# Set differences in two wide pieces, and another order at the ends of the first halves, in a retention and MLP kernel

## The chip, the cores and the metric

One core of a Trainium2 chip runs the whole kernel. The metric is the device time of one execution in microseconds; "before" has the median of three runs. In the profile, PE is TensorE (PEld its weight loads), DVE is VectorE, ACT is ScalarE, POOL is GpSimd, SP is SyncE, whose queue starts the DMAs.

## The reference

```python
# attention with a decaying state, B=2, H=8, S=768, D=64
for t in range(S):
    state = gamma * state + k[t] v[t]^T          # per batch and head
    y[t] = q[t] state / sqrt(D)
x = y as (1536, 512)
h = x @ moe_w_in;  x = silu(h) @ moe_w_out       # 512 -> 2048 -> 512
h = x @ moe2_w_in; out = max(0.01 h, h) @ moe2_w_out
```

Inputs are float32 values; the weights reach the chip as 64-bit words and are decoded there.

## The kernel before, in words

The 1536 tokens are taken in 12 chunks of 128, the two batches by turns. In the attention a chunk j has scores on TensorE (L244), a mask product on VectorE (`masked`, L251), then values, state part and state update on TensorE (`values`, from L254), and on VectorE the state row (L294). `masked(j + 1)` stands ahead of `store_x(j)` and `state(j)` on VectorE. Three chunks make a set of N = 384 tokens, so there are four sets; sets 0 and 1 belong to p = 0, sets 2 and 3 to p = 1. A set's output is needed by the first layer as high and low halves (`halves`: ScalarE copies to fp32r, VectorE subtracts, L178 and L179), because each matrix product is three products of halves: high x high, high x low, low x high.

Each layer has a first half (512 to 2048) in Q = 8 steps, and a second half (2048 to 512) in 3 x 8 steps of 24 matmuls (L453). A step of the first half multiplies 2 x 2 blocks of weights by 2 x 2 blocks of values with seven products instead of eight (`product`, numbers 1 to 7, each 12 matmuls of 384 columns for both p, L376). It takes sums of weight blocks, formed on GpSimd (`sums`, four 128x256 operations, L175), and differences of values between the even and the odd set of a pair p. Of these, L318 and L319 form two on VectorE as soon as a chunk of the odd set is there, and `rest_t` two more on GpSimd over the whole set (L324, L325, 768 columns). `split_t` makes halves of them: 1536 columns on ScalarE and VectorE. Step 0 of a layer (`begin`, L627) does plain blocks instead, 4 blocks x 2 pairs of 12 matmuls (L648), while the differences are still being made; then `n.go(1)` is the first product of step 1. In `rest` (L659) the products of a step stand in a given sequence; `copy` (ScalarE, L405) and `add` (VectorE, L409) collect them, `act` (L418, L420) applies the activation, `keep` (L425) writes the step's output to DRAM scratch, from which `fetch_g` (L441) brings it back for the second half, into `sf` and three tiles `ct`. `split_g` makes its halves.

Weights take five operations before use: `words` (ScalarE, L131 and L133), `clamp` (VectorE, L137 and the mask L141), `sign` (L148), `low` (L155), and the halves. `split_a` and `split_s` are the halves of plain blocks and of sums. Lists of tasks (`up_tasks`, L563; `behind`, L530) say which of these go ahead of which product.

The order is that of the code: engines and the SP queue take their instructions strictly in line, and each instruction waits on semaphores for what it needs. PSUM has four pairs of banks; a pair is a place of one product or of two outputs. The chunk loop ends at L559, the layers' loop follows at L683, and `finish_x` (L458) makes the values of layer 1 from the outputs of layer 0, through `put_first` and `put_second`.

## Time and profile before

| | |
|---|---|
| median of 3 runs | 579.21 us (578.32 to 582.25) |
| profiled execution | 580.35 us, its span 578.6 us |
| mean granted TensorE clock | 0.987 |
| PE busy | 555.2 us, 96% of the span |
| DVE busy | 342.6 us, 59% |
| ACT busy | 282.7 us, 49% |
| POOL busy | 104.4 us, 18% |
| HBM | 80.82 MB read, 37.75 MB written |

The profile is one execution. A busy share is the time an engine spent in its instructions; the chain that ended last is the work followed back from the last instruction through what released each step: 83% of it is TensorE, 6% VectorE, 5% DMA. A row of the timeline gives a start from the span's beginning, a duration, engine, line, operation with output and inputs, their shapes, and how many instructions it joins; in brackets stands how long the engine was idle before, and what released it. Rows of busy time by line and form give the count, the busy time and the mean of one.

### The profile page before, as it was taken

The page shows a single profiled execution, that of the slowest core. Times are in us where ns is not written, and L with a number is a line of the kernel's source. Part 1 is how long each engine was busy: PE and PEld are TensorE (multiplying, and loading weights), DVE is VectorE, ACT ScalarE, POOL GpSimd, SP SyncE. Part 2 cuts the span into 40 slices and gives each one's busy share as a digit, 9 for nine tenths or more (in the row PEclk, how much of TensorE's full clock was granted, in tenths as well). Part 3 has the DMA queues.
Part 4 walks back from the last instruction along what each step waited for, and adds up shares of the span by engine and source line. Part 5 has one row for each costly group of instructions (what it writes and reads, how often), then busy time and mean ns, then how long its engine had stood idle before and what let it go on. Part 6 is the DMA issues. An engine that isn't in the chain of part 4 may idle for free.

```text
span 578.6 us, 7971 instructions
## 1 busy us (share of the span) xinstructions
PE 555.2 (96%) x3246; PEld 498.1 (86%) x3246; DVE 342.6 (59%) x354; ACT 282.7 (49%) x330; POOL 104.4 (18%) x94
## 2 busy tenths in 40 slices
PE   8887979999998999999999899999999999999997
PEld 6776979999997888888888799999998888888885
DVE  4888866888865486676673756666655562212300
ACT  2223566777766565634622565566665453213201
POOL 2675433333300000000200532222200000000000
PEclk9988979999999999999999999999999999999999
DMA  8973216687876957878582075777627782532401
GB/s 323 392 269 116 73 36 219 228 290 283 289 257 237 374 188 215 292 228 311 189 260 105 0 261 175 249 258 252 223 110 290 283 293 94 167 109 84 137 0 73
DMA packets 35129, 119.09 MB, mean 206 GB/s; under 512 B 3218, under 2 KB 3346, under 8 KB 33044
## 3 DMA queue, kind: packets, MB, share of 16 engines
q1 hardware_dynamic: 34800, 118.24, 58.8%
q8 instruction: 25, 0.41, 0.3%
q10 hardware_dynamic: 292, 0.34, 0.2%
q14 instruction: 12, 0.10, 0.1%
HBM read 80.82 MB, written 37.75 MB: 205 GB/s over the span
## 4 chain that ended last, share of the span: by engine, by line
PE 83%; DVE 6%; DMA 5%; ACT 3%; POOL 1%; issue 1%; SPq 0%; DVEq 0%; ACTq 0%
PE p L453 44%; PE p L376 33%; DMA sf<-g 3%; DMA att_a<-att_dram 3%; PE p L648 2%; DVE w L179 2%; POOL sf L175 1%; PE p L273 1%; PE p L264 1%; ACT w L178 1%; PE p L244 1%; DVE c L251 1%; DVE r L155 1%; DVE big L318 1%; DVE big L319 1%
## 5 line engine op out<-in xcount | busy, mean ns | idle before, releaser
L376 PE MATMUL p<-tt,w 128*128 128x384 f32 x672 | 126.3, 340 | 3.7 <-ACT c L405 3.7
L376 PEld LDWEIGHTS p<-tt,w 128*128 128x128 f32 x672 | 119.4, 190 | 5.3 <-ACT c L405 5.2
L179 DVE TENSOR_TENSOR w<-c,w 128x1024 fp32r<-128x1024 f32 x46 | 56.2, 1224 | 90.2 <-ACT w L178 90.1
L453 PE MATMUL p<-w,wt 128*128 128x512 f32 x432 | 98.4, 389 | 0.0
L453 PE MATMUL p<-wt,w 128*128 128x512 f32 x432 | 98.4, 389 | 0.0
L453 PEld LDWEIGHTS p<-wt,w 128*128 128x128 f32 x432 | 81.1, 188 | 16.8
L453 PEld LDWEIGHTS p<-w,wt 128*128 128x128 f32 x432 | 81.1, 188 | 16.8
L178 ACT ACTIVATE w<-c 128x1024 fp32r<-128x1024 f32 x46 | 48.4, 1061 | 60.0 <-DMA c<-g 34.4
L453 PE MATMUL p<-w,w 128*128 128x512 f32 x288 | 67.3, 391 | 1.8 <-DVE w L179 1.0
L376 PE MATMUL p<-xa,w 128*128 128x384 f32 x336 | 64.3, 341 | 2.1 <-ACT big L418 2.1
L453 PEld LDWEIGHTS p<-w,w 128*128 128x128 f32 x288 | 53.8, 188 | 14.3 <-DVE w L179 2.2
L376 PEld LDWEIGHTS p<-xa,w 128*128 128x128 f32 x336 | 59.8, 190 | 2.5 <-ACT big L418 2.5
L409 DVE TENSOR_TENSOR big<-p,c 128x768 f32<-128x768 f32 x42 | 40.1, 954 | 32.3 <-PE p L376 19.8
L405 ACT ACTIVATE c<-p 128x768 f32<-128x768 f32 x42 | 34.1, 812 | 48.7 <-PE p L376 48.6
L175 POOL TENSOR_TENSOR sf<-r 128x256 f32<-128x256 f32 x28 | 33.9, 1232 | 115.6 <-DVE r L155 61.1
L133 ACT ACTIVATE u<-ws 128x1024 int32<-128x1024 uint32 x32 | 36.4, 1137 | 22.5 <-DVE r L155 22.5
L155 DVE CUSTOM_DVE_ANT_0 r<-r,u 128x2048 uint16<-128x2048 uint16 x32 | 41.2, 1289 | 0.9 <-ACT u L133 0.5
L131 ACT ACTIVATE r<-ws 128x1024 f32<-128x1024 f32 x32 | 36.6, 1143 | 9.7 <-DMA scr<-r 5.5
L179 DVE TENSOR_TENSOR w<-sf,w 128x1024 fp32r<-128x1024 f32 (+1 forms) x18 | 21.7, 1205 | 32.8 <-ACT w L178 32.8
L148 DVE SCALAR_TENSOR_TENSOR r<-ws,r 128x1024 int32<-128x1024 int32 x32 | 39.6, 1236 | 0.7
L324 POOL TENSOR_TENSOR big<-big 128x768 f32<-128x768 f32 x4 | 7.3, 1832 | 169.1 <-DVE big L319 169.1
L179 DVE TENSOR_TENSOR w<-r,w 128x768 fp32r<-128x768 f32 (+1 forms) x20 | 23.5, 1175 | 14.5 <-ACT w L178 14.5
(86 smaller groups left out, 566.0 us busy)
## 6 DMA issues: line engine op xcount, KB each, us to landing
ws<-w_dram SPq DMA_DIRECT2D x64, 512.0 KB, 5.7
g<-big SPq DMA_DIRECT2D x16, 1536.0 KB, 5.8
c<-g SPq DMA_DIRECT2D x46, 512.0 KB, 6.8
att_a<-att_dram SPq DMA_DIRECT2D x18, 512.0 KB, 6.4
scr<-r SPq DMA_DIRECT2D x18, 512.0 KB, 6.4
r<-scr SPq DMA_DIRECT2D x18, 512.0 KB, 7.4
att_b<-att_dram SPq DMA_DIRECT2D x6, 512.0 KB, 8.3
out_dram<-big SPq DMA_DIRECT2D x11, 256.0 KB, 2.1
```

Of the source, the lines that this page charges most:

```text
L131: nc.scalar.activation(out=r.bitcast(F32), in_=t[:, :, :, 1].bitcast(F32), func=AF.Abs)
L133: nc.scalar.activation(out=u, in_=t[:, :, :, 0].bitcast(U32), func=AF.Copy, scale=2.0 ** -29)
L148: nc.vector.scalar_tensor_tensor(out=r, in0=t[:, :, :, 1], scalar=-0x40000000, in1=r, op0=ALU.bitwise_and, op1=ALU.bitwise_or)
L155: nc.vector.tensor_tensor(out=r, in0=r, in1=u, op=ALU.add)
L175: nc.gpsimd.tensor_tensor(out=o, in0=a, in1=b, op=op)
L178: nc.scalar.activation(out=h, in_=s, func=AF.Copy)
L179: nc.vector.tensor_tensor(out=l, in0=s, in1=h.bitcast(F32), op=ALU.subtract)
L376: nc.tensor.matmul(out=o, lhsT=a[:, ta, k * 128:k * 128 + 128], rhs=rhs(p, tb, k), start=(begin and m == 0), stop=(end and m == 5), skip_g ...
L405: nc.scalar.activation(out=ct[n][:, c, 0:N], in_=self.X[:, c, 0:N], func=AF.Copy)
L409: nc.vector.tensor_tensor(out=self.block(f, half, lanes), in0=t[:, c, 0:N], in1=ct[n][:, c, 0:N], op=ALU.add)
L453: nc.tensor.matmul(out=y, lhsT=l, rhs=r, start=(i == 0 and f == 0 and n == 0), stop=(i == Q - 1 and f == 1 and n == 2),)
L648: nc.tensor.matmul(out=places[m][:, p, 0:N], lhsT=a[:, ta, r, k * 128:k * 128 + 128], rhs=x, start=(n_ == 0), stop=(n_ == 11), skip_group_ ...
```

## The change: what it does

1. The differences L318 and L319 are no longer formed chunk by chunk from PSUM. For the odd sets ScalarE copies the chunk's whole output to `tm` after the halves (chunk 5 on; up to chunk 4 VectorE writes the product with the gate straight into the target), and `first_t` then takes both differences over 768 columns with operands in SBUF: for p = 0 on GpSimd at chunk 10, for p = 1 on VectorE at the first block of layer 0. `rest_t(0)` moves to chunk 11, `rest_t(1)` behind the sums of the first block of layer 0. In even sets from chunk 5 on the copy comes after the halves instead of ahead of them. `finish_x` does all halves and then all copies of one output half after the other, and the differences at the end.
2. In `begin` the second pair's blocks stand in another sequence, and the first product of the next step with its copy goes ahead of the last block. The tasks of layer 0's first step are in another order.
3. In the last step of a first half the sequence is 6, 2, 7, 5, 4, 3, and the first fetches and halves of the second half stand earlier.

```diff
--- before.py
+++ after.py
@@ -301,23 +301,19 @@
         return t
 
 
-    def put_first(s, a, b, ys):
+    def put(s, a, b, k):
         p = s // 2
-        f = xf[p][:, :, :, a:b]
-        h, l = (xa[p][:, n].rearrange("p (a k) n -> p a k n", a=2)[:, :, :, a:b] for n in range(2))
-        for i, y in enumerate(ys):
-            halves(h[:, i], l[:, i], y)
-        for i, y in enumerate(ys):
-            nc.scalar.activation(out=f[:, i], in_=y, func=AF.Copy)
-
-    def put_second(s, a, b, ys):
-        p = s // 2
-        f, t = xf[p][:, :, :, a:b], tm[p][:, :, :, a:b]
-        h, l = (xb[p][:, n, :, a:b] for n in range(2))
-        halves(*(t[:, :, a:b] for t in b12[p]), ys[0])
-        nc.vector.tensor_tensor(out=t[:, 0], in0=ys[0], in1=f[:, 0], op=ALU.subtract)
-        nc.vector.tensor_tensor(out=t[:, 1], in0=ys[1], in1=t[:, 0], op=ALU.subtract)
-        halves(h, l, ys[1])
+        if s % 2 == 0:
+            h, l = (xa[p][:, n, 2 * k:2 * k + 2, a:b] for n in range(2))
+            return h, l, xf[p][:, k, :, a:b]
+        h, l = ((b12[p], [xb[p][:, n] for n in range(2)])[k][n][:, :, a:b] for n in range(2))
+        return h, l, tm[p][:, k, :, a:b]
+
+
+    def first_t(p, e):
+        f, t = xf[p], tm[p]
+        e.tensor_tensor(out=t[:, 0], in0=t[:, 0], in1=f[:, 0], op=ALU.subtract)
+        e.tensor_tensor(out=t[:, 1], in0=t[:, 1], in1=t[:, 0], op=ALU.subtract)
 
     def rest_t(p):
         f, t = xf[p], tm[p]
@@ -333,24 +329,18 @@
         a, b = c * C, c * C + C
         y = yu[j][0]
         g4 = lambda t: t.rearrange("p (a k i) -> p a k i", a=2, k=2)
-        kept = False
+        y = g4(y)
+        f = (tm if s % 2 else xf)[s // 2][:, :, :, a:b]
         if j < LATE:
-            kept = s % 2 == 0
-            n = j % 2
-            yg = xf[s // 2][:, :, :, a:b] if kept else sf[:, 2 * n:2 * n + 2].rearrange(
-                "p a (k i) -> p a k i", k=2)
-            nc.vector.tensor_tensor(out=yg, in0=g4(y), in1=g4(G), op=ALU.mult)
-            y = yg
+            nc.vector.tensor_tensor(out=f, in0=y, in1=g4(G), op=ALU.mult)
+            y = f
+        if s % 2 == 0:
+            halves(*(xa[s // 2][:, n].rearrange("p (a k) n -> p a k n", a=2)[:, :, :, a:b] for n in range(2)), y)
         else:
-            y = g4(y)
-        if s % 2 == 0:
-            f = xf[s // 2][:, :, :, a:b]
-            h, l = (xa[s // 2][:, n].rearrange("p (a k) n -> p a k n", a=2)[:, :, :, a:b] for n in range(2))
-            if not kept:
-                nc.scalar.activation(out=f, in_=y, func=AF.Copy)
-            halves(h, l, y)
-        else:
-            put_second(s, a, b, [y[:, 0], y[:, 1]])
+            for k in range(2):
+                halves(*put(s, a, b, k)[0:2], y[:, k])
+        if j >= LATE:
+            nc.scalar.activation(out=f, in_=y, func=AF.Copy)
 
 
     TERMS = ((0, 0), (0, 1), (1, 0))
@@ -456,13 +446,18 @@
             )
 
     def finish_x(s, ya, yb):
-        at = s * T
-        while at < s * T + T:
-            e = min(s * T + T, (at // N + 1) * N)
-            n, a = at // N, at % N
-            c = slice(at - s * T, e - s * T)
-            (put_first if n % 2 == 0 else put_second)(n, a, a + e - at, [ya[:, :, c], yb[:, :, c]])
-            at = e
+        for k, y in ((1, yb), (0, ya)):
+            todo = []
+            at = s * T
+            while at < s * T + T:
+                e = min(s * T + T, (at // N + 1) * N)
+                n, a = at // N, at % N
+                todo.append((y[:, :, at - s * T:e - s * T], *put(n, a, a + e - at, k)))
+                at = e
+            for i, h, l, _ in todo:
+                halves(h, l, i)
+            for i, _, _, f in todo:
+                nc.scalar.activation(out=f, in_=i, func=AF.Copy)
 
     def finish_out(s, m, y):
         j = s * (T // C) + m
@@ -531,7 +526,7 @@
             2: lambda: load_next(), 5: lambda: load_next(),
             4: lambda: words(wa), 6: lambda: clamp(wa), 7: lambda: signed(wa),
             8: lambda: low(wa), 9: lambda: split_a(wa),
-            10: lambda: (rest_t(0), words(wb)), 11: lambda: (rest_t(1), clamp(wb), signed(wb)),
+            10: lambda: (first_t(0, nc.gpsimd), words(wb)), 11: lambda: (rest_t(0), clamp(wb), signed(wb)),
         }
         places = [place(p) for p in range(2)]
         for j in range(NJ):
@@ -566,13 +561,13 @@
             if layer == 0 and k < 2:
                 wd = first_w[3]
                 if k == 0:
-                    at(0, lambda: split_t(0, 0), lambda: low(wb))
-                    at(1, lambda: sums(wb), lambda: split_t(1, 0))
-                    at(2, lambda: split_a(wb))
-                    at(3, lambda: split_t(0, 1), lambda: words(wc))
-                    at(4, lambda: split_s(wb))
-                    at(5, lambda: split_t(1, 1))
-                    at(6, lambda: clamp(wc), lambda: signed(wc))
+                    at(0, lambda: low(wb), lambda: first_t(1, nc.vector), lambda: sums(wb))
+                    at(0, lambda: split_t(0, 0), lambda: rest_t(1))
+                    at(1, lambda: split_a(wb), lambda: split_t(1, 0))
+                    at(3, lambda: split_s(wb), lambda: words(wc))
+                    at(4, lambda: split_t(0, 1))
+                    at(5, lambda: split_t(1, 1), lambda: clamp(wc))
+                    at(6, lambda: signed(wc))
                     at(7, lambda: low(wc), lambda: sums(wc))
                 else:
                     at(0, lambda: split_a(wc))
@@ -605,7 +600,7 @@
             w = second_w[1][k]
             n, m = (first_w[Q + k + d] if k + d < Q else None for d in (1, 2))
             if k == 0:
-                at(0, lambda: split_t(1, 0), lambda: fetch_w(n))
+                at(0, lambda: fetch_w(n), lambda: split_t(1, 0))
                 at(2, lambda: split_a(n), lambda: words(w))
                 at(4, lambda: sums(n), lambda: clamp(w))
                 at(5, lambda: signed(w), lambda: fetch_w(m))
@@ -652,25 +647,28 @@
                             n_ += 1
                     if p == 1:
                         s.act(f, half, places[m])
+                    if p == 1 and at == 2:
+                        n.go(1)
+                        n.copy(0)
                 put_back[p]()
-            n.go(1)
-            n.copy(0)
 
         def rest(s, n, before, tasks):
-            seq = (6, 2, 5, 7, 1, 4, 3) if n else (6, 2, 5, 7, 0, 4, 3)
+            seq = (6, 2, 5, 7, 1, 4, 3) if n else (6, 2, 7, 5, 4, 3)
             for m, p in enumerate(seq):
                 if m == 2:
                     if before.i:
                         before.act(0, 1)
+                    if n is None:
+                        fetch_g(s.layer, 0, 1)
                     before.keep()
-                if p == 7:
+                if m == 3:
                     s.act(0, 0)
                 for t in tasks[m]:
                     t()
                 if p == 1:
                     n.go(1)
                     n.copy(0)
-                elif p:
+                else:
                     s.go(p)
                 if p == 6:
                     s.copy(1)
@@ -678,8 +676,9 @@
                     s.add(0, 0, 0, s.Z)
                 elif p == 7:
                     s.copy(2)
+                if m == 3:
                     s.add(1, 1, 2, s.V)
-                elif p == 4:
+                if p == 4:
                     s.act(1, 1)
                     s.act(1, 0, s.X)
                 elif p == 3:
@@ -694,16 +693,16 @@
                 s, n = steps[k], steps[k + 1]
                 if k == 0:
                     begin(s, n, tasks, ((0, 1, 2, 3), (1, 3, 0, 2))[layer],
-                          ((1, 0, 2, 3), (2, 0, 1, 3))[layer], put_back)
+                          ((0, 1, 2, 3), (0, 2, 1, 3))[layer], put_back)
                     s.done()
                     continue
                 if n is None:
                     ahead = second_w[layer][:2]
-                    tasks[2] += [lambda: fetch_g(layer, 0, 0), lambda: fetch_g(layer, 0, 1)]
-                    tasks[3] += [lambda: fetch_w(ahead[0])]
-                    tasks[4] += [lambda: split_g(layer, 0, 0), lambda: fetch_g(layer, 0, 2)]
-                    tasks[5] += [lambda: fetch_w(ahead[1])]
-                    tasks[6] += [lambda: split_g(layer, 0, 1)]
+                    tasks[1] += [lambda: split_g(layer, 0, 0)]
+                    tasks[2] += [lambda: fetch_w(ahead[0])]
+                    tasks[4] += [lambda: fetch_g(layer, 0, 2), lambda: fetch_w(ahead[1]), lambda: split_g(layer, 0, 1)]
+                elif k == Q - 2:
+                    tasks[4] += [lambda: fetch_g(layer, 0, 0)]
                 rest(s, n, steps[k - 1], tasks)
             steps[Q - 1].act(0, 1)
             fetch_g(layer, 0, 3)
@@ -791,6 +790,7 @@
                         put_back[1] = lambda: free.append(last_place)
                     finish_x(s, ya, yb)
                     if s:
+                        first_t(s - 1, (nc.gpsimd, nc.vector)[s - 1])
                         rest_t(s - 1)
                 elif end_:
                     for m in range(4):
```

On VectorE, in chunks 8 and 9 of the attention (p_555, now p_550, is the output of chunk 9, `gst` the state). Before:

```order
L294 TENSOR_TENSOR gst<-gst,p_512 128x256 [waits Pool_49]
L155 ISA r_74<-r_74,u 128x2048 [waits DVE_49]
L251 TENSOR_TENSOR c_70<-p_544,c_69 128x1024 [waits PE_49]
L179 TENSOR_TENSOR w_87<-p_555,w_87 128x2x128 [waits Activation_49]
L318 TENSOR_TENSOR big<-p_555,big 128x2x128
L319 TENSOR_TENSOR big<-p_555,big 128x2x128 [waits DVE_49]
L179 TENSOR_TENSOR xb_67<-p_555,xb_67 128x2x128 [waits Activation_49]
L294 TENSOR_TENSOR gst<-gst,p_555 128x256 [waits Pool_49]
L179 TENSOR_TENSOR w_88<-r_74,w_88 128x1024 [waits Activation_49]
L251 TENSOR_TENSOR c_71<-p_591,c_69 128x1024 [waits PE_49]
```

Now:

```order
L294 TENSOR_TENSOR gst<-gst,p_507 128x256 [waits Activation_49,Pool_49]
L155 ISA r_74<-r_74,u 128x2048 [waits DVE_49]
L251 TENSOR_TENSOR c_70<-p_539,c_69 128x1024 [waits PE_49]
L179 TENSOR_TENSOR w_87<-p_550,w_87 128x2x128 [waits Activation_49]
L179 TENSOR_TENSOR xb_67<-p_550,xb_67 128x2x128 [waits Activation_49]
L294 TENSOR_TENSOR gst<-gst,p_550 128x256 [waits Activation_49,Pool_49]
L179 TENSOR_TENSOR w_88<-r_74,w_88 128x1024 [waits DVE_49,Activation_49]
L251 TENSOR_TENSOR c_71<-p_585,c_69 128x1024 [waits PE_49]
```

The two differences are gone, and the state rows wait for ScalarE as well as for GpSimd; that wait is for the copy of the same output.

On ScalarE, in the start of layer 0 (`w_659` and `w_651` are halves of sums, `tt_658` and `tt_650` those of the second pair's differences, `big<-p` the silus of the blocks). Before:

```order
L178 ACTIVATE w_89<-r_75 128x768 [waits DVE_49]
L178 ACTIVATE tt_85<-big 128x2x768 [waits Pool_49]
L131 ACTIVATE r_76<-ws_72 128x1024 [waits DMAHW7_49,DMAHW6_49]
L133 ACTIVATE u<-ws_72 128x1024 [waits Activation_49]
L178 ACTIVATE w_659<-sf 128x1024 [waits Pool_49]
L418 ACTIVATE big<-p_662 128x2x384 [waits DVE_49,PE_49]
L178 ACTIVATE tt_658<-big 128x2x768
L418 ACTIVATE big<-p_661 128x2x384 [waits PE_49]
L418 ACTIVATE big<-p_663 128x2x384 [waits PE_49]
L418 ACTIVATE big<-p_664 128x2x384 [waits PE_49]
L405 ACTIVATE c_69<-p_794 128x2x384 [waits PE_49]
```

Now:

```order
L178 ACTIVATE w_89<-r_75 128x768 [waits DVE_49]
L178 ACTIVATE tt_650<-big 128x2x768 [waits DMAHW4_49,DMAHW5_49,DMAHW3_49,DMAHW6_49,DMAHW2_49,DMAHW7_49,DVE_49,Activation_49]
L178 ACTIVATE w_651<-sf 128x1024 [waits Pool_49]
L131 ACTIVATE r_76<-ws_72 128x1024 [waits DMAHW7_49,DMAHW6_49]
L133 ACTIVATE u<-ws_72 128x1024
L178 ACTIVATE tt_85<-big 128x2x768
L408 ACTIVATE big<-p_653 128x2x384 [waits DVE_49,PE_49]
L178 ACTIVATE tt_650<-big 128x2x768 [waits Pool_49]
L408 ACTIVATE big<-p_654 128x2x384 [waits PE_49]
L408 ACTIVATE big<-p_655 128x2x384 [waits PE_49]
L395 ACTIVATE c_69<-p_772 128x2x384 [waits PE_49]
L408 ACTIVATE big<-p_656 128x2x384 [waits PE_49]
```

The first silu stood behind the halves of the sums; now the halves of both pairs' differences `tt_85` and `tt_650` stand around it, and the copy of the next product (L395) stands ahead of the last silu.

On GpSimd, the end of the attention and the start of layer 0 (`att_b` is the last chunk's input, `r_75` the first weights). Before:

```order
L222 TENSOR_TENSOR att_b<-att_b,gst 128x512 [waits DMAHW4_49,PE_49]
L324 TENSOR_TENSOR big<-big 128x768 [waits Activation_49]
L325 TENSOR_TENSOR big<-big 128x768
L324 TENSOR_TENSOR big<-big 128x768 [waits DVE_49,Activation_49]
L325 TENSOR_TENSOR big<-big 128x768
L175 TENSOR_TENSOR sf<-r_75 128x256 [waits DVE_49]
L175 TENSOR_TENSOR sf<-r_75 128x256
L175 TENSOR_TENSOR sf<-sf,r_75 128x256 [waits Pool_49]
L175 TENSOR_TENSOR sf<-r_75,sf 128x256 [waits Pool_49]
```

Now:

```order
L222 TENSOR_TENSOR att_b<-att_b,gst 128x512 [waits DMAHW4_49,PE_49]
L315 TENSOR_TENSOR big<-big 128x768 [waits Activation_49]
L316 TENSOR_TENSOR big<-big 128x768 [waits Pool_49]
L320 TENSOR_TENSOR big<-big 128x768 [waits Pool_49]
L321 TENSOR_TENSOR big<-big 128x768
L175 TENSOR_TENSOR sf<-r_75 128x256 [waits DVE_49]
L175 TENSOR_TENSOR sf<-r_75 128x256
L175 TENSOR_TENSOR sf<-sf,r_75 128x256 [waits Pool_49]
L175 TENSOR_TENSOR sf<-r_75,sf 128x256 [waits Pool_49]
L320 TENSOR_TENSOR big<-big 128x768 [waits DVE_49,Activation_49]
L321 TENSOR_TENSOR big<-big 128x768
```

L315 and L316 are the new wide differences, L320 and L321 are `rest_t`: that of the second pair moved from ahead of the four sums to behind them.

## Rows read from the trace of the kernel before

**Rows 1.** The page's line of TensorE's granted clock: 40 slices of 14.5 us, tenths.
```profile
PEclk9988979999999999999999999999999999999999
```

**Rows 2.** TensorE's waits: line waited for, us in total, times, longest us.
```profile
PE p L264 <- DVE c L251: 7.0, 4, 2.8
PE p L376 <- ACT c L405: 3.7, 4, 1.0
...
PE p L648 <- DVE xb L179: 2.7, 1, 2.7
```

**Rows 3.** Windows: bounds, us, busy by engine, granted clock, DMA share, GB/s.
```profile
80.00:84.00 4.00, 3.10 (x10) 2.59 (x10) 3.90 (x5) 2.07 (x3) 0.00 (x0) 0.50 0.01 4
322.00:330.00 8.00, 5.33 (x31) 5.04 (x31) 6.67 (x6) 4.99 (x5) 4.77 (x3) 1.00 0.00 0
```

**Rows 4.** Timeline, one mask operation at two places: start us, us, engine, line, operation.
```profile
63.00 2.22 DVE L141 TENSOR_SCALAR r<-r 128x1024 int32<-128x1024 int32 x1
...
177.92 0.69 DVE L141 TENSOR_SCALAR r<-r 128x1024 int32<-128x1024 int32 x1
```

**Rows 5.** Groups by line and form: count, busy us, mean ns, idle before.
```profile
L318 DVE TENSOR_TENSOR big<-sf,big 128x256 f32<-128x256 f32 x2 | 2.8, 1375 | 0.0
L319 DVE TENSOR_TENSOR big<-sf,big 128x256 f32<-128x256 f32 x2 | 1.6, 786 | 0.1
L318 DVE TENSOR_TENSOR big<-p,big 128x768 f32<-128x768 f32 x1 | 0.9, 948 | 0.0
L324 POOL TENSOR_TENSOR big<-big 128x768 f32<-128x768 f32 x4 | 7.3, 1832 | 169.1 <-DVE big L319 169.1
L178 ACT ACTIVATE tt<-big 128x1536 fp32r<-128x1536 f32 x8 | 11.6, 1478 | 0.0
```

**Rows 6.** Timeline, attention: ScalarE's copy of an output, and the last mask product.
```profile
44.84 0.60 ACT L350 ACTIVATE big<-p 128x512 f32<-128x512 f32 x1 [2.67 <-PE p L281]
...
53.88 1.22 DVE L251 TENSOR_TENSOR c<-p,c 128x1024 f32<-128x1024 f32 x1
```

**Rows 7.** Timeline, start of layer 0, several engines.
```profile
66.40 1.75 DVE L179 TENSOR_TENSOR tt<-big,tt 128x1536 fp32r<-128x1536 f32 x1
68.07 1.22 DVE L155 CUSTOM_DVE_ANT_0 r<-r,u 128x2048 uint16<-128x2048 uint16 x1
...
75.26 0.73 POOL L175 TENSOR_TENSOR sf<-r,sf 128x256 f32<-128x256 f32 x1
...
77.83 3.44 PE L376 MATMUL p<-xa,w 128*128 128x384 f32 x12 [2.14 <-ACT big L418]
...
85.93 2.26 PE L376 MATMUL p<-xa,w 128*128 128x384 f32 x12
```

**Rows 8.** Timeline, ends of the two first halves (layers 0 and 1).
```profile
176.01 1.12 ACT L133 ACTIVATE u<-ws 128x1024 int32<-128x1024 uint32 x1
176.13 4.35 PE L376 MATMUL p<-tt,w 128*128 128x384 f32 x24
...
187.85 8.50 PE L453 MATMUL p<-w,w 128*128 128x512 f32 x36 [0.76 <-DVE w L179]
...
433.54 4.35 PE L376 MATMUL p<-tt,w 128*128 128x384 f32 x24
...
443.78 6.60 PE L453 MATMUL p<-w,w 128*128 128x512 f32 x26 [0.25 <-DVE w L179]
```

**Rows 9.** Timeline, start of layer 1, several engines.
```profile
318.56 0.38 ACT L178 ACTIVATE xa<-p 128x256 fp32r<-128x256 f32 x1 [0.97 <-PE p L453]
...
319.72 0.81 ACT L178 ACTIVATE w<-p 128x768 fp32r<-128x768 f32 x1
...
323.52 1.82 POOL L324 TENSOR_TENSOR big<-big 128x768 f32<-128x768 f32 x1 [42.34 <-DVE big L319]
...
332.61 1.60 POOL L175 TENSOR_TENSOR sf<-r,sf 128x256 f32<-128x256 f32 x1
...
341.15 2.38 PE L376 MATMUL p<-tt,w 128*128 128x384 f32 x12 [0.90 <-ACT c L405]
```

## The prediction, made before the changed kernel ran

> **What bounds the kernel now.** I read the slices first. TensorE is busy in nearly every one, and the line of its granted clock stays at 9 outside three slices [rows 1]: products at full clock fill the program, and time can be won or lost only where TensorE waits or runs at half clock. The waits of TensorE say where that is [rows 2]: on the mask product of VectorE in the attention (7.0 us), on copies by ScalarE in the product steps (3.7 us), and once on a low half of VectorE (2.7 us). The edits touch four such places: the attention with the start of layer 0, the last step of layer 0, the start of layer 1, its last step. The rest of the program moves as a block.
>
> Two facts of the trace set the prices. The first is the clock. In 80 to 84 us it was 0.50, the 1.2 GHz level, after TensorE had stood 2.14 us in front of a product [rows 3, 7]; in 322 to 330 us it was 1.00, the 2.4 GHz level, though 2.67 of the 8 us were idle [rows 3]. So some waits cost a stretch at half clock on top and some don't. The second is that VectorE and GpSimd hold each other up: the same mask of a word tile (L141) took 2.22 us while GpSimd subtracted and 0.69 us with GpSimd idle [rows 4]. A chunk's difference with both inputs in SBUF took 1375 ns as a mean [rows 5]. The Trainium skill has a rule for this ("SBUF — State Buffer", section "Who interferes with whom"): a VectorE instruction with two SBUF inputs and a GpSimd instruction that reads SBUF lock each other out for a whole instruction, and one with a PSUM input is free of that. It speaks against this change, which replaces differences from PSUM by differences of two SBUF operands.
>
> **The sum.** All times are on the profiled execution's scale, 580.35 us, of which 578.6 is the span; the median of the three runs is 1.14 lower.
>
> *Attention.* The two-operand differences of chunks 3 and 4 go: 2 x (1.375 + 0.786) = 4.3 us [rows 5]. They stood ahead of the state row and the next mask product on VectorE. One low half then waits out part of a GpSimd product, so I take -4.1. In return ScalarE copies a whole output from chunk 5 on, 0.60 us each [rows 6], behind its halves, and the state row on VectorE, which before waited for GpSimd alone, now waits for that copy too; behind the state row the next mask product is queued, and for that TensorE waits. In chunk 5 copy and removed differences cancel (-0.2); in 6, 7 and 8 it costs 0.6 each (+1.9); in 9 about half (+0.3). The wide differences on GpSimd at chunk 10 can catch a VectorE instruction for up to one of their 1.83 us [rows 5]: half of that, +0.9. The last mask product, which ended at 55.10 [rows 6], ends at 53.9: -1.2, between -3.7 and -0.4.
>
> *Start of layer 0 up to the low words.* From the last mask product to the end of the low words (69.29) [rows 7] passed 14.2 us. Out of this go four differences, a 1.75 us low half of a set [rows 7], and the hold on the masks of the words (1.53 on L141 by [rows 4], about 1 on the clamp before it, an estimate from the same two rows); two ScalarE copies come in at 0.60. That leaves 9.5 us: -4.7.
>
> *From there to the first product of the next step.* Here the cover is gone. Behind the low words now stand, all with SBUF operands and so one after the other on VectorE and GpSimd: two wide differences (0.95 each, [rows 5]), four sums (0.73, [rows 7]), two low halves of sets (1.75), two remaining differences (1.83, [rows 5]) and two low halves of weights (about 1.2, as the low words): 14.4 us. Each starts some 0.07 before the last ends (66.40 + 1.75 against 68.07), so 13.6. ScalarE takes its orders in line: the silu that frees the first product's PSUM place stands behind the high half of the last difference, so 1.48 [rows 5] and 0.8 for the silu follow (768 columns, as [rows 9]): 15.9. Before it was 77.83 - 69.29 = 8.5: +7.4. Moving the product ahead of the last block does not fill the gap, since the product itself waits for that silu. It starts at 79.3 and not at 77.83.
>
> By the skill's rule that issue order decides who blocks, VectorE would win where it asks first, and the window would be 12.5, the sum 1.1 lower. No row shows an order of that kind beyond strict alternation, so I keep 13.6.
>
> *From that product on.* Before, 8.1 us passed from 77.83 to the third product at 85.93 [rows 7], 3.0 of them by the half clock, for two products of 2.1 and a copy of 0.9. Now three pieces go there (product, block, product), 6.3, and the copy is covered. The clock will fall again, for the wait is about 7 us. The least that a slice at 8 tenths stands for is 1.5 us lost [rows 1]; the most seen here is 3.0. I take 2.5: 8.8, +0.7. Start of layer 0 and attention in all: +2.2, between -2.4 (mask product at its low end, 1.5 lost, issue order) and +3.5.
>
> *Last step of layer 0.* From 176.13 four products should end at 184.5; the run of the second half starts at 187.85 [rows 8], so 3.1 are lost, to a copy between two products and to the halves of the first fetched values. The new order puts another product between copy and overwrite, and fetches a step earlier. New is that product 3 waits for an add on VectorE, behind the low half of the fetched values, the masks and the signs. ScalarE's word pass ends at 177.13 [rows 8] and the half behind it at 178.2; then 1.2, 0.95, 0.69, 0.69, 1.2 and the add's 0.95 on VectorE give 183.9, against 182.4 when TensorE gets there: 1.5 of wait. Net -1.6, between -3.1 and -0.5.
>
> *Last step of layer 1.* Same reading: 433.54 + 8.4 = 441.9, the run starts at 443.78 after one lone product [rows 8], about 1.5 lost. Here the words stand behind the fetched values and the add is early: -1.5, between -1.5 and 0.
>
> *Start of layer 1.* The first difference on GpSimd started at 323.52, since each piece was finished in turn. Now all halves and copies of both outputs come first: per output, ScalarE and VectorE by turns with 0.38, 0.43, 0.81 and 0.96, then copies of 0.39 and 0.81, 3.8 us, twice with handovers 7.9 from 318.56 [rows 9]; the 768-wide half of 0.81 is in the rows, the 256-wide ones are the first row of the group and near it. Then two wide differences on VectorE, 1.9: GpSimd starts at 328.4, 4.9 later. From there 11.1 us of exclusive work as above (two differences 3.7, one low half 1.75, weights 0.95, sums 2.9, masks 1.4, signs 1.2, less overlaps 0.8) end at 339.5; they ended at 334.21 [rows 9]. Then 1.05 + 1.48 + 0.81 + 0.81 on ScalarE: product 6 at 343.7, against 341.15: +2.5. TensorE has the product and the last block to fill with, and still idles about 4.8 us in front of product 6. That lies between 2.67 idle, after which the clock stayed, and 7, so half clock costs 0 to 3.0, and I take 1.6: +4.1.
>
> The sum is +2.2 - 1.6 - 1.5 + 4.1 = +3.2: 583.6 on the profile's scale, **582.4 against the median**, +0.6%. About 1% is what a measurement of this kernel can tell from no change, that is 573.4 to 585.0. All terms low give 574.7, all high 587.7.
>
> **Rivals.**
>
> *The shared work isn't one after the other (faster), 0.20.* If GpSimd's long operations ran beside VectorE's, only their own chain would count: low words at 63.4, then sums 2.9 and differences 3.7, then 1.48 and 0.8: the product starts at 72.2, the clock holds, and the next step's second piece of work, at 85.93 before, is reached at 78.5: -7.4. In layer 1, 328.4 + 3.7 + 2.9 + 4.2 = 339.2: -2.0 and no half clock. With -1.6 and -1.5 that is -12.5: 567.9, 566.7 against the median. For it speaks that a mean in the rows mixes calm and crowded cases; against it speak the two times of L141 [rows 4].
>
> *Both new waits cost a full stretch at half clock (slower), 0.27.* The place is the three pieces behind the 7 us wait in layer 0, and the product behind the 4.8 us wait in layer 1. If all 6.3 us behind the first run at 1.2 GHz, that is 3.8 more than I took, and 3.0 behind the second is 1.4 more: 588.8, 587.6 against the median. For it speaks that 2.14 us of waiting was enough once [rows 3]; against it, that 2.67 was not. It is slower by over 1% from 2.6 us of half clock loss above my 4.1.
>
> *The forecast, 0.53.* Its upper terms alone reach past 585.0 in a tenth of its cases, and its lower ones below 573.4 in fewer.
>
> The range is 570 to 589: it takes in both ends of the forecast and the slower rival and leaves out most of the faster one. Faster by over 1%: 0.20 + 0.03 = 0.23. Slower: 0.27 + 0.06 = 0.33, within 1%: 0.44.
>
> **What the changed profile would show.** The last mask product ends near 53.9. Between the low words and the first silu of layer 0, VectorE and GpSimd alternate without overlap for some 13 us, and TensorE shows one wait of about 7 us in front of the first product (by the line of ACT's silu); if that wait is under 3, the faster rival holds. The clock's fall behind it lasts 3 to 6 us; over 7 is the slower one. In the last step of layer 0 product 3 waits 1.5 for an add. In layer 1 GpSimd's differences start near 328, product 6 near 343.7 less what was won before. I would be wrong altogether if a DMA, which I took as in time everywhere, were the last to come: the fetches moved a step earlier stand on SP's queue ahead of others.

## The result, and the profile after

The change makes the kernel slower: 588.12 us (median of 4, 587.3 to 588.73) against 579.95 for the kernel before beside it, a ratio of 1.0137 with the interval 1.0098 to 1.0176. The profiled execution took 588.43 us, its span 586.6 us, 8.0 more than before. The granted clock is no explanation by itself: 0.985 against 0.987, and the page's line answers to [rows 1].

```profile
PEclk9998979999999999999999999999999999999999
```

TensorE's waits after, as in [rows 2]:

```profile
PE p L264 <- issue: 5.8, 3, 4.4
PE p L366 <- ACT big L408: 4.6, 1, 4.6
PE p L366 <- ACT c L395: 4.0, 2, 3.7
PE p L443 <- DVE w L179: 2.4, 2, 1.6
...
```

A row with `issue` has no releaser in the profile; its longest wait, 4.4 us, ends where the last mask product of the attention does (54.41 and 54.31 us). In its second halves the kernel before had three short waits (L443 is what L453 was), all at the start: 0.70 and 0.76 us in layer 0, 0.25 in layer 1 [rows 8]. Now there is a row of them, and their place is seen when TensorE's runs of layer 0's second half are set side by side. Before (start us, us, what, how many; idle before and its end):

```profile
186.59 0.49 PE L453 MATMUL p<-w,w 128*128 128x512 f32 x1 [0.70 <-ACT w L178]
187.85 10.99 PE L453 MATMUL p<-w,w 128*128 128x512 f32 x47 [0.76 <-DVE w L179]
198.68 32.80 PE L453 MATMUL p<-w,wt 128*128 128x512 f32 x144
...
242.20 32.80 PE L453 MATMUL p<-w,wt 128*128 128x512 f32 x144
...
285.72 32.80 PE L453 MATMUL p<-w,wt 128*128 128x512 f32 x144
```

After:

```profile
188.21 11.04 PE L443 MATMUL p<-w,w 128*128 128x512 f32 x48
199.71 0.81 PE L443 MATMUL p<-w,wt 128*128 128x512 f32 x2 [0.46 <-ACT wt L178]
201.16 16.68 PE L443 MATMUL p<-w,wt 128*128 128x512 f32 x72 [0.64 <-DVE wt L179]
218.30 16.20 PE L443 MATMUL p<-w,wt 128*128 128x512 f32 x70 [0.46 <-DVE wt L179]
234.34 11.04 PE L443 MATMUL p<-w,w 128*128 128x512 f32 x48
246.06 0.50 PE L443 MATMUL p<-w,wt 128*128 128x512 f32 x1 [0.68 <-ACT w L178]
247.31 32.69 PE L443 MATMUL p<-w,wt 128*128 128x512 f32 x143 [0.76 <-DVE w L179]
...
298.53 27.27 PE L443 MATMUL p<-w,wt 128*128 128x512 f32 x119 [1.65 <-DVE w L179]
```

Three unbroken sets of 43.5 us became three broken ones. With the same marks in both traces (start of a named run, after minus before) the 8.0 us fall apart so:

| stretch | shift at its end | its own share |
|---|---|---|
| attention and start of layer 0, to the third product (85.93, now 87.64) | +1.7 | +1.7 |
| layer 0's steps, to the last step (176.13, now 178.44) | +2.3 | +0.6 |
| last step of layer 0, to the second half (187.62 without its lone first matmul, now 188.21) | +0.6 | -1.7 |
| second half of layer 0 (318.36, now 325.63) | +7.3 | +6.7 |
| start of layer 1, to its third product (343.37, now 353.51) | +10.1 | +2.9 |
| steps of layer 1, to the last step (433.54, now 443.85) | +10.3 | +0.2 |
| last step of layer 1 (443.55 without its lone first matmul, now 452.21) | +8.7 | -1.7 |
| to the end | +8.0 | -0.7 |

The largest share lies in a stretch for which the forecast had no term. The first two rows set one execution against one: profiles of runs with the same code up to there reach the second half of layer 0 up to 1.7 us apart (187.36 us in e5, 189.06 in e1), so these two shares are known no better than that.

### The profile page after: what moved, and what is told of

The parts are those of the page before. It is cut to its first block, busy times and chain, and to the rows that moved or that the text cites. A ratio compares the mean times of both kernels' runs of the same rounds, so it can differ in the third digit from the quotient of the medians.

```text
span 586.6 us, 7977 instructions
## 1 busy us (share of the span) xinstructions
PE 557.8 (95%) x3246; PEld 499.8 (85%) x3246; DVE 342.8 (58%) x340; ACT 288.0 (49%) x340; POOL 116.0 (20%) x98
## 4 chain that ended last, share of the span: by engine, by line
PE 59%; DVE 12%; DMA 10%; ACT 8%; issue 6%; POOL 4%; SPq 0%; ACTq 0%; DVEq 0%; POOLq 0%
PE p L366 30%; PE p L443 27%; DMA c<-g 5%; DVE r L155 3%; DMA att_a<-att_dram 2%; ACT w L178 2%; DVE w L179 2%; POOL sf L175 2%; DMA att_b<-att_dram 1%; DMA scr<-r 1%; DVE r L141 1%; DVE r L148 1%; DVE r L137 1%; POOL big L321 1%; DVE xa L179 1%
## 5 line engine op out<-in xcount | busy, mean ns | idle before, releaser
L179 DVE TENSOR_TENSOR w<-c,w 128x1024 fp32r<-128x1024 f32 x46 | 57.6, 1256 | 97.8 <-ACT w L178 97.6
L443 PE MATMUL p<-w,wt 128*128 128x512 f32 x432 | 100.3, 391 | 4.7 <-DVE w L179 2.4
L443 PEld LDWEIGHTS p<-w,wt 128*128 128x128 f32 x432 | 80.6, 188 | 24.2 <-DVE w L179 3.6
L443 PE MATMUL p<-wt,w 128*128 128x512 f32 x432 | 98.4, 389 | 0.0
L443 PEld LDWEIGHTS p<-wt,w 128*128 128x128 f32 x432 | 81.1, 188 | 16.8
L443 PE MATMUL p<-w,w 128*128 128x512 f32 x288 | 66.3, 389 | 0.0
L443 PEld LDWEIGHTS p<-w,w 128*128 128x128 f32 x288 | 54.0, 188 | 11.1
L395 ACT ACTIVATE c<-p 128x768 f32<-128x768 f32 x42 | 34.0, 811 | 44.7 <-PE p L366 44.6
L155 DVE CUSTOM_DVE_ANT_0 r<-r,u 128x2048 uint16<-128x2048 uint16 x32 | 42.8, 1339 | 0.9 <-ACT u L133 0.7
L179 DVE TENSOR_TENSOR w<-sf,w 128x1024 fp32r<-128x1024 f32 x16 | 21.3, 1329 | 33.1 <-ACT w L178 33.1
L179 DVE TENSOR_TENSOR w<-r,w 128x768 fp32r<-128x768 f32 (+1 forms) x20 | 26.2, 1312 | 16.7 <-ACT w L178 16.7
L366 PE MATMUL p<-xb,w 128*128 128x384 f32 x168 | 31.7, 337 | 1.2 <-DVE big L399 1.2
```

The costliest lines, as they stand in the source:

```text
L155: nc.vector.tensor_tensor(out=r, in0=r, in1=u, op=ALU.add)
L179: nc.vector.tensor_tensor(out=l, in0=s, in1=h.bitcast(F32), op=ALU.subtract)
L366: nc.tensor.matmul(out=o, lhsT=a[:, ta, k * 128:k * 128 + 128], rhs=rhs(p, tb, k), start=(begin and m == 0), stop=(end and m == 5), skip_g ...
L395: nc.scalar.activation(out=ct[n][:, c, 0:N], in_=self.X[:, c, 0:N], func=AF.Copy)
L443: nc.tensor.matmul(out=y, lhsT=l, rhs=r, start=(i == 0 and f == 0 and n == 0), stop=(i == Q - 1 and f == 1 and n == 2),)
```

## The experiments

The median of every run with the ratio to the kernel before, which ran beside it:

| run | us | ratio (95%) |
|---|---|---|
| the change | 588.12 | 1.0137 (1.0098 to 1.0176) |
| e1_old_finish | 581.16 | 1.002 (1.0001 to 1.0038) |
| e2_keep_first | 586.52 | 1.0109 (1.0076 to 1.0143) |
| e3_old_last | 588.9 | 1.0151 (1.0111 to 1.0191) |
| e4_split_late | 588.63 | 1.0145 (1.0107 to 1.0182) |
| e5_first_vec | 587.72 | 1.0135 (1.0104 to 1.0166) |
| e6_only_last_kf | 576.68 | 0.9948 (0.9923 to 0.9974) |
| e7_finish_keep | 578.42 | 0.997 (0.9948 to 0.9992) |
| e8_no_first0 | 586.17 | 1.011 (1.0072 to 1.0148) |
| e9_by_piece | 578.2 | 0.9936 (0.9916 to 0.9957) |
| e10_ahead | 576.42 | 0.991 (0.9888 to 0.9933) |
| e11_state_first | 586.79 | 1.0095 (1.0068 to 1.0122) |
| e12_hybrid | 575.1 | 0.9923 (0.99 to 0.9947) |

**e1_old_finish: layer 1's values formed as before.**

```diff
     def finish_x(s, ya, yb):
-        for k, y in ((1, yb), (0, ya)):
...
+            (put_first if n % 2 == 0 else put_second)(n, a, a + e - at, [ya[:, :, c], yb[:, :, c]])
...
-                        first_t(s - 1, (nc.gpsimd, nc.vector)[s - 1])
```

> The change, but with the kernel before's way of forming layer 1's values: each piece with its two differences at once on VectorE from PSUM, no wide differences there. Theory 1: the second half of layer 0 loses 6.7 us at three separate places, 2.4 by a late train of fetches at its start, 2.0 where the first output set is turned into values, 2.3 where the wide differences run on GpSimd; the last two go, and the 2.9 of layer 1's start go too, so 588.1 - 7.2 = 580.9. Theory 2: the late train alone pushes the half off its pace, and the two later waits only follow from it; then the second half stays at about +6 and only layer 1's start is won back, 588.1 - 2.9 = 585.2.

Measured 581.16: theory 1. The waits at 200 and 219 us stay, those near 246 and 298 are gone. Layer 0's second half takes 133.0 us (189.06 to 322.09) where the change takes 137.4 (188.21 to 325.63). So the larger part of the loss sits in how the values are formed, and not in a late train of fetches alone.

**e2_keep_first: the second fetch behind the write.**

```diff
-                    if n is None:
-                        fetch_g(s.layer, 0, 1)
                     before.keep()
+                    if n is None:
+                        fetch_g(s.layer, 0, 1)
```

> The change, but in the last steps the second fetch stands behind the write of the step before and not ahead of it on the DMA queue. Theory 1: the write leaves some 5 us earlier, the third fetch lands before it is wanted, the two waits near 200 us go: 588.1 - 2.4 = 585.7, and the waits near 246 and 298 us stay. Theory 2: all three go, 588.1 - 6.7 = 581.4.

The two waits near 200 us and the one near 218 are gone, those behind stay: theory 1. The first set in this run is whole:

```profile
200.81 32.80 PE L443 MATMUL p<-w,wt 128*128 128x512 f32 x144
```

In time it is 586.52, 1.6 less, and the two intervals overlap. The trace shows more: the second half of layer 0 takes 133.9 us (189.93 to 323.84) and not 137.4, so 3.5 less, but this profile reaches it 1.7 later, and 1.2 of that stand already at layer 0's first block (59.44 against 58.22), in code that both share. What happened is in the DMA engines' strip over 176 to 200 us (tenths busy, 40 slices of 0.6 us). Before:

```profile
DMA  0000779989946999999989989999669999999899
```

After:

```profile
DMA  9400000000000926999999979999889989999999
```

For some 7 us from 177 on nothing moves (in the kernel before, nothing moves up to 178.4). The second fetch stands at the head of SP's queue and waits for a tile that VectorE's add still reads (181.56 to 182.51); behind it wait the 1.5 MB write and every other transfer. So ScalarE's halves of the third values come late. Before, the write's issue and those halves:

```profile
177.89 0.33 SPq L425 DMA_DIRECT2D g<-big  x1
...
193.12 1.06 ACT L178 ACTIVATE w<-c 128x1024 fp32r<-128x1024 f32 x1 [1.19 <-DMA c<-g]
```

After:

```profile
183.20 0.55 SPq L415 DMA_DIRECT2D g<-big  x1
...
197.65 1.06 ACT L178 ACTIVATE w<-c 128x1024 fp32r<-128x1024 f32 x1 [5.31 <-DMA c<-g]
```

In this run the write leaves 7.1 us ahead of the second half (182.86 to 189.93), in the change 5.0 (183.20 to 188.21): 2.1 earlier and not the 5 that were expected. That is enough for the three waits.

**e3_old_last: the last steps as before, all else changed.** The edit puts back the sequence 6, 2, 5, 7, 0, 4, 3 and the old places of fetches and halves.

> The change, but with the last steps' sequence, fetches and halves of the kernel before. Theory 1: the last step's gain is given up in both layers (+1.7 and +1.65), the late train of fetches in layer 0 goes (-2.4), and the end gets back 0.65 that it had won: 588.1 + 1.6 = 589.7. Theory 2 (all of the second half's loss hangs on the fetches): 588.1 + 3.35 - 6.7 = 584.8.

Measured 588.9, nearer to theory 1 (589.7): the last steps win about as much as the late train loses. A miss in detail: the waits near 246 went too, only that near 296 stayed (1.47). There the fetched values were halved at 231.73, ahead of the forming of layer 1's values, and 1.7 us earlier than in the change (233.61) at nearly the same place of TensorE. A late train is not the reason by itself, for in e2 it is repaired and the waits near 246 stay. What differs is the lead over TensorE: the halves start 2.5 us ahead of TensorE's next set here (234.20), 0.9 in e2 (232.52, 233.45) and 0.7 in the change (234.34). With the old last step TensorE comes later, and the forming of the values has more slack.

**e4_split_late: the silu no longer behind the last halves in layer 0's first step.**

```diff
-                    at(5, lambda: split_t(1, 1), lambda: clamp(wc))
+                    at(5, lambda: clamp(wc))
...
+                    at(7, lambda: split_t(1, 1))
```

> The change, but in layer 0's first step the halves of the second pair's last differences come behind the next step's first product, so that the silu which frees its place no longer stands behind them on ScalarE. Theory 1 (the wait of 4.65 us is that place in line): the product starts at about 76.5 instead of 78.8, -2.3, and with less waiting some of the half clock goes, -0 to -2: 583.8 to 585.8. Theory 2 (the window of VectorE and GpSimd itself is the limit, and the silu would wait for sums or halves anyway): no change, 588.1.

TensorE in this run, at the product and at the new wait:

```profile
77.14 4.21 PE L366 MATMUL p<-xa,w 128*128 128x384 f32 x12 [4.14 <-ACT big L408]
...
95.30 2.37 PE L366 MATMUL p<-tt,w 128*128 128x384 f32 x12 [0.93 <-ACT c L395]
```

The product starts 1.6 us earlier (78.76 in the change), but the wait in front of it shrinks by only 0.5; the other 1.1 lie ahead of the wait, where the code is the same. A new wait of 0.93 appears later. The time, 588.63, is not less. The place in line was real, but it alone isn't worth anything that was measured: here the silu waits for GpSimd's last difference (0.87 us, L321), as theory 2 has it.

**e5_first_vec: the first pair's wide differences on VectorE in the forming of layer 1's values.** The edit is `first_t(s - 1, nc.vector)`.

> The change, but in the making of layer 1's values the first pair's wide differences run on VectorE instead of GpSimd. Theory 1: the wait of 1.65 us near 298 and what lies around it comes from VectorE's low words and low halves being held by GpSimd's four long operations; two of the four go, and VectorE has 2 x 0.95 us more to do in line: between -2.3 (all of it) and -0.5, about 586.5. Theory 2: the place is late because ScalarE and VectorE work by turns on the outputs, whoever takes the differences: the wait stays, 588.1 or up to 1.9 more.

TensorE's two waits in this run at the place where the change has the one of 1.65:

```profile
290.78 5.74 PE L443 MATMUL p<-w,wt 128*128 128x512 f32 x24 [0.55 <-DVE w L179]
297.01 27.29 PE L443 MATMUL p<-w,wt 128*128 128x512 f32 x119 [0.50 <-DVE w L179]
```

One wait of 1.65 became two of about half a microsecond, the time is the same: theory 2. In sum TensorE waits 0.6 less there, so GpSimd's hold on VectorE has a part in it; that it makes the place late by itself was a wrong reading, as e9 shows better.

**e6_only_last_kf: the kernel before with the repaired last steps alone.** The sequences, fetches and halves of the last steps from the change, with e2's edit, in the kernel before.

> The kernel before, with the new sequence, fetches and halves of the last steps alone, and the second fetch behind the write on the DMA queue. Theory 1 (the last step's order is a gain by itself, its only harm is the fetch ahead of the write): 580.2 - 1.7 - 1.65 = 576.8, no wait in the second half of layer 0. Theory 2 (the earlier start of the second half is lost again to fetches and decoding that set its pace): 579 to 580.

576.68, ratio 0.9948: theory 1, with no wait between 190 and 318 us.

**e7_finish_keep: e1 and e2 together.**

> The change with both repairs: layer 1's values formed as in the kernel before, and the second fetch behind the write. If the effects of the two add up: 581.2 - 1.6 = 579.6, with no wait of TensorE left between 190 and 320 us. If they cover each other, 581.

578.42: in time the effects add up, if anything a little more, and no wait is left in the second half of layer 0. That half takes 130.6 us (189.75 to 320.31), as in the kernel before (130.7 by the marks of the table). So the 6.7 are explained by the two causes, and in part they cover each other: 3.5 (e2) and 4.4 (e1) are 7.9.

**e8_no_first0: the first pair's differences left out of the attention.**

> The change without the first pair's four differences in the attention (the wide ones at chunk 10 and the two behind them are left out, so products with them use other data). Theory 1 (GpSimd's long operations hold VectorE's low half and low words there): the low half of 2.58 us falls to 1.2 and the low words of 2.22 to 1.2, the last mask product ends near 51.9 instead of 54.3. Theory 2 (inputs that land late, or the copies on ScalarE, set that chunk): it stays within 0.5 of 54.3.

VectorE in this run, the weights' low half and the last mask product behind it:

```profile
49.96 1.22 DVE L179 TENSOR_TENSOR w<-r,w 128x1024 fp32r<-128x1024 f32 x1 [0.46 <-ACT w L178]
51.10 1.22 DVE L251 TENSOR_TENSOR c<-p,c 128x1024 f32<-128x1024 f32 x1
```

The low half, 2.58 us in the change (50.59 to 53.17), is 1.22 here, and the last mask product ends at 52.32 and not at 54.31: theory 1, 2.0 us. In the other eight profiles with this attention the product ends at 54.23 to 55.53, so 52.32 is clear of them. The low words kept 2.21, but those were held by another GpSimd operation, the query scaling (43.66, 1.27 us).

**e9_by_piece: e2, and both outputs of a piece side by side where layer 1's values are formed.**

```diff
-        for k, y in ((1, yb), (0, ya)):
-            todo = []
-            at = s * T
-            while at < s * T + T:
+        at = s * T
+        while at < s * T + T:
...
+            todo = [(y[:, :, at - s * T:e - s * T], *put(n, a, a + e - at, k)) for k, y in ((0, ya), (1, yb))]
             for i, h, l, _ in todo:
                 halves(h, l, i)
```

> The change with the second fetch behind the write, and in the making of layer 1's values the pieces one after the other with both outputs side by side, as the kernel before had them, instead of one output after the other; the wide differences stay where the change has them. Theory 1 (one output at a time leaves ScalarE waiting for VectorE at every step): the two waits near 245 us go, the one near 296 stays: 586.5 - 2.0 = 584.5. Theory 2 (the copies that the change adds fill ScalarE there, in whatever order): no change, 586.5.

Far more than either theory: 578.2, ratio 0.9936, below the kernel before. All waits of layer 0's second half are gone, that near 296 too; the set in which the change waits at 246 is whole:

```profile
243.32 32.80 PE L443 MATMUL p<-w,wt 128*128 128x512 f32 x144
```

Against e2's trace layer 0's second half is 3.3 us shorter (130.6 and 133.9). The larger part of the gain lies behind it, where neither theory had looked: from layer 1's first block to its third product pass 23.2 us (319.48 to 342.68) where e2 has 28.0 (323.84 to 351.88). GpSimd's differences start 6.5 us behind the first block and not 9.8 as in the change, and the wait in front of product 6 is 1.15 and not 3.70. In the second half GpSimd holds VectorE as before:

```profile
282.74 1.85 POOL L320 TENSOR_TENSOR big<-big 128x768 f32<-128x768 f32 x1
282.83 2.84 DVE L179 TENSOR_TENSOR w<-c,w 128x1024 fp32r<-128x1024 f32 x1 [1.62 <-ACT w L178]
284.54 2.83 POOL L321 TENSOR_TENSOR big<-big 128x768 f32<-128x768 f32 x1
```

The hold is what the Trainium skill says of two SBUF inputs beside GpSimd ("SBUF — State Buffer", section "Who interferes with whom"), and the trace agrees: 2.84 where the same half takes 1.23 alone. But it costs TensorE nothing here. What costs is the turns of ScalarE and VectorE on one output. In the change:

```profile
234.56 0.79 ACT L178 ACTIVATE xa<-p 128x768 fp32r<-128x768 f32 x1
...
239.41 0.38 ACT L178 ACTIVATE xb<-p 128x256 fp32r<-128x256 f32 x1 [4.05 <-DVE xa L179]
240.28 1.09 ACT L460 ACTIVATE big<-p 128x768 f32<-128x768 f32 x2 [0.49 <-DVE xb L179]
241.25 0.82 ACT L178 ACTIVATE xa<-p 128x768 fp32r<-128x768 f32 x1
...
243.09 0.39 ACT L178 ACTIVATE b<-p 128x256 fp32r<-128x256 f32 x1 [1.02 <-DVE xa L179]
243.97 1.09 ACT L460 ACTIVATE big<-p 128x768 f32<-128x768 f32 x2 [0.49 <-DVE b L179]
244.94 1.06 ACT L178 ACTIVATE w<-c 128x1024 fp32r<-128x1024 f32 x1
```

In e9_by_piece:

```profile
232.46 1.50 ACT L178 ACTIVATE xa<-p 128x768 fp32r<-128x768 f32 x2
...
237.31 1.68 ACT L457 ACTIVATE big<-p 128x768 f32<-128x768 f32 x2 [3.35 <-DVE xa L179]
...
240.37 1.05 ACT L178 ACTIVATE w<-c 128x1024 fp32r<-128x1024 f32 x1
```

Between two instructions on one PSUM tile ScalarE waits for VectorE in these rows. With one output at a time every step is such a wait, and the fetched values `c` get their halves 10.4 us after the first output's (234.56 to 244.94); with two outputs side by side ScalarE works on one while VectorE works on the other, and it is 7.9 (232.46 to 240.37). ScalarE's idle time accounts for the whole difference: 6.05 us in the change, 3.57 in e9 (the long waits of 4.05 and 3.35 are mostly VectorE's masks and signs, which stand in line in both). TensorE needs those halves, and where the change reaches them there is no slack of 2.5 us. The edit also takes the outputs in the other order and copies each piece ahead of the next; no run separates that from the turns.

The wide differences themselves are no loss here: layer 1's first half takes 122.5 us in e9 (319.48 to 441.98) and 123.9 in e7 (320.31 to 444.21), where the differences are formed as in the kernel before and the rest of layer 1 is the same.

**e10_ahead: e6, and the next step's first product ahead of the last block in both layers.**

```diff
                     if p == 1:
                         s.act(f, half, places[m])
+                    if p == 1 and at == 2:
+                        n.go(1)
+                        n.copy(0)
                 put_back[p]()
-            n.go(1)
-            n.copy(0)
```

> The kernel before with the new last steps (second fetch behind the write) and, in both first steps, the next step's first product and its copy ahead of the last block; tasks and the sequence of blocks as before. Theory 1: the block covers the copy's 0.90 us in both layers, and in layer 0 the wait for the silu stays: 576.7 - 0.2 - 0.9 = 575.6. Theory 2 (what stands behind is late anyway, so the cover wins nothing): 576.7.

576.42, ratio 0.991 against e6's 0.9948; the intervals overlap, so by the times alone the two can't be told apart. In the trace the copy's wait of 0.90 in layer 1 is gone, and from layer 1's first block to product 6 pass 23.2 us (315.90 to 339.09) where e6 has 24.35 (315.38 to 339.73): 1.2, as theory 1 has it.

**e11_state_first: in the attention the copy behind the state row.** The edit issues `state(j)` ahead of ScalarE's copy.

> The change, but in the attention ScalarE's copy of an output stands behind the state row of VectorE, which so waits for GpSimd alone. Theory 1 (each copy of 0.60 us delays the state row and the next mask product): the last mask product ends 1.9 us earlier, near 52.4, and the time is 588.1 - 1.5 = 586.6. Theory 2 (input that lands late and GpSimd's long operations set those chunks): it stays near 54.3, 588.1.

The last mask product in this run:

```profile
52.12 1.21 DVE L251 TENSOR_TENSOR c<-p,c 128x1024 f32<-128x1024 f32 x1
```

The last mask product ends 1.0 us earlier (53.33), half of what theory 1 wanted, and 0.9 ahead of the earliest of the profiles with the change's attention (54.23). The time is 586.79, and its interval overlaps that of the change. GpSimd's operations have a part in the rest (e8), and so has input that lands late: in this run GpSimd's query scaling waits 2.04 us for a DMA at 39.96.

**e12_hybrid: e10 with e9's way of forming layer 1's values.**

> Attention and start of layer 0 as in the kernel before; from the change the new last steps (second fetch behind the write), the next step's first product ahead of the last block, and the wide differences in the making of layer 1's values, there with both outputs of a piece side by side. Theory 1 (piece by piece the wide differences are a gain at layer 1's start, where from its first block to product 7 pass 25.3 us and not 27.4): 1.5 to 2 us less than the kernel without them, a ratio to the kernel before of 0.988. Theory 2 (the gain there is lost again in the second half, where GpSimd's long operations hold VectorE): 0.991 as without them.

575.1, ratio 0.9923, not to be told from e10's 0.991. In the trace layer 1's start is shorter, 24.9 us from its first block to product 7 (316.71 to 341.64) against 27.4 in e10 (315.90 to 343.26), and the second half has no wait. Layer 1's whole first half is 1.8 shorter (316.71 to 438.75, and 315.90 to 439.70), and layer 0's second half takes 130.6 in both, so the gain isn't lost there as theory 2 has it. The span is only 0.9 us shorter, since this run reaches layer 0's second half 0.8 later. The trace speaks for theory 1, the times don't settle it; either version beats both kernels.

## Why the prediction was right in its parts and 5.7 us short

The time lies in the forecast's range, on the side of the slower cases (0.33), and the likeliest case, no change, did not come. That it lies inside is luck: the range reached so high for the slower rival's sake (587.6), and that rival's cause, a long fall of the clock, did not come; the steps that had a price came to less than forecast, and what filled the range is a loss without a term. By the steps of the prediction:

- **What bounds the kernel: "the rest of the program moves as a block" failed.** The stretch that it was to cover lost 6.7 us. The second half of layer 0 holds two of the three places at which `finish_x` works, and it starts with the fetches that were moved. The prediction priced the new `finish_x` once, at the start of layer 1, and not at the first two sets, where the same turns stand ahead of the halves that TensorE needs (e1, e9). The queue of fetches stood in its last sentence as a way to be wrong, without a price (e2).
- **Attention, -1.2; measured -0.8** (54.31 against 55.10), **which isn't a gain that is shown.** In the four profiles with the attention of before (before, e6, e10, e12) the last mask product ends at 53.38 to 55.10, and the one that the forecast started from is the latest; with the change's it ends at 54.23 to 55.53 in eight profiles. The gain in chunks 3 and 4 came: the mask product of chunk 6 starts at 27.77 and before at 31.75. What it had won was lost again behind it. A DMA was not in time there, as the forecast took it to be everywhere, and TensorE waited 1.24 us for this operation:

```profile
41.09 1.67 POOL L222 TENSOR_TENSOR att_a<-att_a,gst 128x512 f32<-128x512 f32 x1 [4.03 <-DMA att_a<-att_dram]
```

The collision with GpSimd took 2.0 (e8) where 0.9 stood, and the copies ahead of the state rows 1.0 (e11) where 1.9 stood for chunks 6 to 8.
- **Up to the low words, 9.5 us; measured 9.58** (54.31 to 63.89). These rows of after answer to [rows 6, 7]:

```profile
53.10 1.21 DVE L251 TENSOR_TENSOR c<-p,c 128x1024 f32<-128x1024 f32 x1
...
62.67 1.22 DVE L155 CUSTOM_DVE_ANT_0 r<-r,u 128x2048 uint16<-128x2048 uint16 x1
...
78.76 4.21 PE L366 MATMUL p<-xa,w 128*128 128x384 f32 x12 [4.65 <-ACT big L408]
...
87.64 2.25 PE L366 MATMUL p<-xa,w 128*128 128x384 f32 x12
```

- **From there to the product, 15.9; measured 14.9** (63.89 to 78.76, forecast 79.3). VectorE and GpSimd took turns throughout, as the forecast had it; the faster rival is out. GpSimd's last difference ended at 76.49, 12.6 behind the low words, where 13.6 stood; 12.5 was the prediction's figure for the other order, but the engines still alternate, so the nearness says nothing for it. The three pieces took 8.9 (8.8 forecast). In all +1.7 for +2.2. The wait itself is 4.65 and not 7, since TensorE too reached the place later than I had counted: behind the wait for the last mask product its clock was 0.50 over 54 to 60 us, where it was 0.72 before.
- **Last step of layer 0, -1.6; measured -1.7.** Product 3 waits 1.15 for the add (1.5 forecast); TensorE after, as in [rows 8]:

```profile
178.44 6.43 PE L366 MATMUL p<-tt,w 128*128 128x384 f32 x36
186.02 2.35 PE L366 MATMUL p<-xb,w 128*128 128x384 f32 x12 [1.15 <-DVE big L399]
```

- **Last step of layer 1, -1.5; measured -1.7**, without a wait, as [rows 8] were read.
- **Start of layer 1, +4.1; measured +2.9.** GpSimd's differences came 4.7 us later relative to the first block (4.9 forecast), product 6 1.5 later (2.5). After, as in [rows 9]:

```profile
335.45 1.85 POOL L320 TENSOR_TENSOR big<-big 128x768 f32<-128x768 f32 x1 [38.06 <-DVE big L316]
...
349.92 3.79 PE L366 MATMUL p<-tt,w 128*128 128x384 f32 x12 [3.70 <-ACT c L395]
353.51 2.43 PE L366 MATMUL p<-xa,w 128*128 128x384 f32 x12
```

- **Half clock, 2.5 and 1.6.** It came behind both waits and stayed short, so the slower rival as I priced it is out too: 0.61 and 0.66 of the clock in these stretches (columns as in [rows 3]). The three pieces took 2.6 us more than their 6.3, product 6 and the start of the next 1.5 more than 2.1 (349.92 to 353.51).

```profile
78.00:86.00 8.00, 7.24 (x27) 7.24 (x28) 5.55 (x6) 2.49 (x5) 2.13 (x4) 0.61 0.29 97
349.00:354.00 5.00, 4.08 (x14) 4.08 (x15) 3.09 (x3) 2.67 (x5) 1.46 (x3) 0.66 0.80 298
```

The forecast's four terms sum to +3.2, and the same four stretches measured +1.2, the first of them between single executions. The 6.8 that make up the rest are +6.7 in the second half of layer 0 and +0.1 over the steps of both layers (+0.6, +0.2) and the end (-0.7).

## What to carry to other kernels

A helper that is changed for one place is changed at all its calls: price the change at each, and look there for who is queued behind it. Two engines that hand one tile to and fro wait for each other at each turn; give them two tiles to alternate on. That order alone took the kernel here from 586.52 (e2) to 578.2 us (e9). And a transfer placed early in an in-order queue is early only if what it waits for is early: it holds everything behind it.

## What the runs showed of the hardware that was not expected

What a hold between VectorE and GpSimd costs depends on what waits behind it, not on its length: the low half of 2.84 us in e9 kept TensorE waiting nowhere, one of 2.58 us in the attention of the change was most of the 2.0 us that e8 won back.

And the length of a wait did not by itself tell whether the clock falls. Behind the wait of 2.67 us at layer 1's start the profile of before kept the full clock [rows 3], and the forecast built on that. In e6 the code there is the same and so is the wait, and the clock fell to 0.66 over 322 to 327 us:

```profile
322.37 2.09 PE L648 MATMUL p<-b,w 128*128 128x384 f32 x6 [2.66 <-DVE xb L179]
...
322.00:327.00 5.00, 4.63 (x18) 4.66 (x19) 4.58 (x4) 3.45 (x4) 2.15 (x2) 0.66 0.00 0
```

It fell behind this wait in e1, e7 and e10 too (0.65, 0.55 and 0.61 of the clock). One execution that kept its clock was no measure of what such a wait costs.
